# Delta-rule attention and a Mish layer on one core: heads paired over batches b and b+2, attention stages of half a chunk in five bundles, and TensorE's order written out

## The chip, the cores and the metric

The kernel runs on one core of one Trainium2 chip. The metric is the device time of one execution in microseconds. Before the change the median of three runs is 741.32 us (740.75 to 742.46). The profiled execution has a span of 745.6 us.

The engines are named as in the profile: PE is TensorE (matrix products; PEld are its weight loads), DVE is VectorE, ACT is ScalarE, POOL is GpSimd and SP is SyncE, which issues the DMAs.

## The reference, cut to what matters

```python
# q, k, v: (4, 8, 768, 48) float32, beta: (4, 8, 768); batch, head, token, dimension
k_n = k / (np.linalg.norm(k, axis=-1, keepdims=True) + 1e-06)
state = zeros((B, H, D, D))
for t in range(S):
    y[:, :, t] = einsum('bhd,bhde->bhe', q[:, :, t], state)
    v_old = einsum('bhde,bhd->bhe', state, k_n[:, :, t])
    state = state + beta[:, :, t, None, None] * einsum('bhd,bhe->bhde', k_n[:, :, t], v[:, :, t] - v_old)

x = y.transpose(0, 2, 1, 3).reshape(4 * 768, 8 * 48)      # 3072 tokens of 384
h = x @ w_in                                              # 384 x 2048
sp = where(h > 20, h, log1p(exp(minimum(h, 20))))
out = (h * tanh(sp)) @ w_out                              # 2048 x 384
```

The weights come as float64. The first part is a recurrence over the tokens for each of 32 heads of a batch; the second works on each token alone.

## The kernel before, in words

**Chunks.** The 768 tokens are cut in 12 chunks of 64. A chunk has 4 batches x 64 = 256 tokens for the Mish layer. Layer n, on chunk n, runs while the attention of chunk n+1 runs; the y of chunk n+1 has to be complete when layer n+1 begins.

**The layer** (`moe`) makes eight pieces g1 and eight pieces g2. A g1 is 18 products into an h tile of 128x512 in PSUM (line L505; 128x256 a product, in float32r with high and low parts), and then a chain: exp on ACT (L509), add on DVE (L510), square, log and exp on ACT (L511 to L513), a scalar-tensor-tensor e<-e,h on DVE (L514, the last reader of h), a cast to g on ACT (L522) and the low part of g on DVE, or on POOL in the first three layers (L525). A g2 is 12 products of 128x384 into two accumulators (L535) and comes two pieces after its g1. The h tiles have two buffers in PSUM, so an h begins when e<-e,h of the h before the last one is done. At a layer's end `turn` transposes the next chunk's y to x (L481, L483, L484).

**The attention of a chunk** (`step`) has five stages. Two heads side by side share every instruction; before the change these are heads 2p and 2p+1 of one batch, and a stage works on one batch (PB = 4 pairs).

- s1: v scaled on POOL (L361), q transposed on DVE (L372), products gq with K and the state (64x64 tiles, L381), v less a part of them (L386), another part masked into xx (L389)
- s2: za = T~ times v for the first 32 tokens (32x32 tiles, L398), copied to xx on ACT (L403)
- s3: pr (32x32, L413), v less pr on DVE (L419)
- s4: zb as za, for the other 32 tokens
- s5: py and ps, the output y and the new state (128x64 and 128x48, L431 and L437), copied out on ACT (L446, L447); the next chunk's k is loaded into xx

The four batches go through the stages one behind the other. All small PSUM tiles come from a pool `at` with four buffers.

**The early part of a group of two chunks** (`early`): K transposed on DVE (L216), Gram blocks pg on PE (64x32, L235), a forward substitution of 31 steps on DVE (L290, L295; for group 1 the first 18 steps are on POOL), which gives T~ in tt (L301). Stages s2 and s4 read tt.

**What sets the order.** `plan` gives each piece a time in units of a layer; pieces are emitted in the order of their times, and a scheduler then orders each engine's instructions by its own estimate of time, unless they stand within `manual_schedule` for that engine. `m0, m1` bound the stretch of times that does; with (9, 9) it is empty.

Of the kernel before, what the change touches and what calls it, by code (L numbers as in the profile page):

```python
# [16 lines left out]
# float32 values whose bits are 0x38000000 and 0x47EFFFFF: the high words of float64s of  # L17
# float32's least and largest exponent
# [15 lines left out]
def kernel(  # L34
# [32 lines left out]
    P = 128  # L67
# [3 lines left out]
    PB = NP // B  # L71
# [5 lines left out]
    kk = k.rearrange("b (p hh) t d -> hh t (b p) d", hh=2)  # L77
    qq = q.rearrange("b (p hh) t d -> hh t (b p) d", hh=2)
    vv = v.rearrange("b (p hh) t d -> hh t (b p) d", hh=2)
    bt = beta.rearrange("b (p hh) (g t2 c i) -> hh c t2 (b p) g i", hh=2, t2=2, c=2, i=32)  # L80
# [20 lines left out]
    # lmask[p, f] = f >= p % 32 ; amask[(hh,c,j), i] = i > 32c + j  # L101
# [21 lines left out]
    # parts of the weights, each first as float64 and then, in the same place, as high and low parts  # L123
# [47 lines left out]
    def convert(kind, i):  # L171
# [5 lines left out]
        # magnitudes outside float32's exponents go to 0 or the largest  # L177
        # and 2^-80 of the rest has bits that, moved up by 3, are float32's of -|w|
# [5 lines left out]
        # the sign comes by VectorE or, while VectorE is what holds the start up, by the others  # L184
# [18 lines left out]
    kts, tts, nes, ats, vts, dts, tus, yms = {}, {}, {}, {}, {}, {}, {}, {}  # L203

    def early(g):
# [3 lines left out]
        for t2 in range(2):  # L209
# [57 lines left out]
        # N[i, j] = -G[i, j] b'_j ; X = (I - N)^-1 in place  # L267
# [42 lines left out]
    def merge(n):  # L310
        """T~'s rows 16.. and columns ..15 of each block of 32: -T~22 G21 T~11."""
# [39 lines left out]
    def load_k(n, b):  # L351
        for hh in range(2):
            load(xx[b][64 * hh:64 * hh + 64, :, hh, D + C:], kk[hh, C * n:C * n + C, PB * b:PB * b + PB])

    def step(n, y):
        g, t2 = n // 2, n % 2
        kt, at, ne = kts[n], ats[n], nes[g]

        def scale_v(b):
            vt = vts[n, b // 2][:, PB * (b % 2):PB * (b % 2) + PB, :]  # L360
            nc.gpsimd.tensor_tensor(out=vt, in0=vt,  # L361
                                    in1=bcast_in(ne[:, 16 * t2 + PB * b:16 * t2 + PB * b + PB], D), op=ALU.mult)

        def s1(b, half=None):
            pr = slice(PB * b, PB * b + PB)
            p8 = slice(PB * (b % 2), PB * (b % 2) + PB)
            vt, x = vts[n, b // 2], xx[b]
            if n:
                scale_v(b)
            for hh in range(2 if half != 1 else 0):  # L370
                r = slice(64 - 64 * hh, 128 - 64 * hh)
                queue(nc.vector.transpose(x[r, :, hh, D:D + C], qsrc[r, pr].rearrange("p a b c -> p a (b c)")), n == 0)  # L372
            if half == 0:
                return
            # S is 0 in the first chunk
            d = D if n else 0
            ps = pa.tile([P, PB, C + d], F32, tag="at", name=f"gq{n}_{b}")
            for p in range(PB):
                for hh in range(2):
                    r = slice(64 - 64 * hh, 128 - 64 * hh)  # L380
                    m = nc.tensor.matmul(ps[64 * hh:64 * hh + 64, p, :], kt[r, PB * b + p], x[r, p, hh, D - d:D + C],  # L381
                                         start=True, stop=True)
            if n == 0:
                keep_warm(TN.get('wgq', 1), m)
            if n:
                nc.vector.tensor_tensor(out=vt[:, p8, :], in0=vt[:, p8, :], in1=ps[:, :, 0:D], op=ALU.subtract)  # L386
            for hh in range(2):
                r = slice(64 * hh, 64 * hh + 64)
                queue(nc.vector.tensor_tensor(out=x[r, :, hh, D:D + C], in0=ps[r, :, d:],  # L389
                                              in1=bcast_mid(amask[r], PB), op=ALU.mult), n < QS)  # L390

        def solve(b, c):
            """Z~ of the chunk's tokens 32c.."""
            pz = pa.tile([P, PB, D], F32, tag="at", name=f"z{"ab"[c]}{n}_{b}")
            for p in range(PB):
                for hh in range(2):
                    r = slice(64 * hh + 32 * c, 64 * hh + 32 * c + 32)
                    m = nc.tensor.matmul(pz[r, p, :], tts[g][r, t2, PB * b + p, :],  # L398
                                         vts[n, b // 2][r, PB * (b % 2) + p, :], start=True, stop=True)
# [339 lines left out]
```

## Time and profile before

| what | us |
|---|---|
| median of three runs | 741.32 (740.75 to 742.46) |
| profiled execution, span | 745.6 |
| first h product of layers 0, 1, 2, 3 | 93.1, 163.5, 230.5, 289.1 |
| of layers 4 to 8 | 341.6, 393.9, 446.4, 498.6, 551.1 |
| of layers 9, 10, 11 | 602.0, 652.5, 700.3 |

The profiled execution is 4.3 us longer than the median. In the timeline a row is a run of equal instructions: start, duration from the first one's start to the last one's end, engine, line, operation, output<-inputs, tile of PE (rows x columns), shape, count, and in brackets the idle time before it and what ended it. A float32 product leaves two records, a float32r product one. In the rows that group a line, the numbers behind the bar are busy time, mean ns of one, idle time before them and its releasers.

### The profile page before, as it was taken

The page shows a single profiled execution, that of the slowest core. Times are in us where ns is not written, and L with a number is a line of the kernel's source. Part 1 is how long each engine was busy: PE and PEld are TensorE (multiplying, and loading weights), DVE is VectorE, ACT ScalarE, POOL GpSimd, SP SyncE. Part 2 cuts the span into 40 slices and gives each one's busy share as a digit, 9 for nine tenths or more (in the row PEclk, how much of TensorE's full clock was granted, in tenths as well). Part 3 has the DMA queues.
Part 4 walks back from the last instruction along what each step waited for, and adds up shares of the span by engine and source line. Part 5 has one row for each costly group of instructions (what it writes and reads, how often), then busy time and mean ns, then how long its engine had stood idle before and what let it go on. Part 6 is the DMA issues. An engine that isn't in the chain of part 4 may idle for free.

```text
span 745.6 us, 22768 instructions
## 1 busy us (share of the span) xinstructions
PE 682.3 (92%) x9656; PEld 602.3 (81%) x9674; DVE 534.3 (72%) x1152; ACT 468.9 (63%) x1005; POOL 127.4 (17%) x171
## 2 busy tenths in 40 slices
PE   5659699878799989999999999999999999999993
PEld 3236588768788878998898998998988989989993
DVE  5796999997747997659995579975499964454351
ACT  2233667755485666776776767767767767767681
POOL 3431336894221221000000000000000000000000
PEclk9756999789899999999999999999999999999998
DMA  5762910253213032122222221130130120000000
GB/s 87 185 181 40 380 32 7 30 84 60 25 32 59 8 54 48 21 44 50 37 34 41 40 38 34 24 51 15 24 59 14 33 49 18 18 23 1 17 7 21
DMA packets 160981, 37.75 MB, mean 51 GB/s; under 512 B 154224, under 2 KB 157296, under 8 KB 160880
## 3 DMA queue, kind: packets, MB, share of 16 engines
q1 hardware_dynamic: 160880, 36.30, 24.0%
q8 instruction: 76, 1.25, 0.7%
q14 instruction: 25, 0.20, 0.1%
HBM read 31.56 MB, written 4.72 MB: 49 GB/s over the span
## 4 chain that ended last, share of the span: by engine, by line
PE 67%; DVE 20%; SPq 4%; issue 3%; ACT 2%; DMA 2%; POOL 1%; DVEq 0%; POOLq 0%; ACTq 0%
PE h L505 24%; PE acc L535 22%; PE gq L381 4%; SPq L131 3%; PE py L431 3%; PE pg L235 2%; PE za L398 2%; DVE pr L290 2%; PE zb L398 2%; PE pr L413 2%; DVE gt L295 2%; PE warm L570 2%; PE ps L437 2%; DVE e L514 1%; DVE xx L389 1%
## 5 line engine op out<-in xcount | busy, mean ns | idle before, releaser
L505 PE MATMUL h<-x,wi 128*128 128x256 f32 x1728 | 238.3, 291 | 13.5 <-DVE e L514 12.1
L505 PEld LDWEIGHTS h<-x,wi 128*128 128x128 f32 x1728 | 218.4, 192 | 23.8 <-DVE e L514 12.5
L535 PE MATMUL acc<-wo,g 128*128 128x384 f32 x1152 | 233.4, 350 | 2.3 <-ACT g L522 1.9
L535 PEld LDWEIGHTS acc<-wo,g 128*128 128x128 f32 x1152 | 201.1, 192 | 8.8 <-ACT g L522 2.5
L514 DVE SCALAR_TENSOR_TENSOR e<-e,h 128x512 f32<-128x512 f32 x96 | 65.8, 685 | 45.5 <-ACT e L513 43.9
L522 ACT CAST g<-e 128x512 fp32r<-128x512 f32 x96 | 59.3, 618 | 49.6 <-DVE e L514 48.6
L361 POOL TENSOR_TENSOR vt<-vt,ne 128x192 f32<-128x192 f32 x48 | 27.3, 589 | 351.9 <-DMA vt<-in_v_dram 187.1
L509 ACT ACTIVATE e<-h 128x512 f32<-128x512 f32 x96 | 57.2, 596 | 47.9 <-PE h L505 45.2
L511 ACT ACTIVATE e<-e 128x512 f32<-128x512 f32 x96 | 60.5, 631 | 33.0 <-DVE e L510 32.5
L510 DVE TENSOR_SCALAR e<-e 128x512 f32<-128x512 f32 x96 | 42.7, 446 | 32.2 <-ACT e L509 31.0
L525 DVE TENSOR_TENSOR g<-e,g 128x512 fp32r<-128x512 f32 x72 | 49.1, 681 | 19.2 <-ACT g L522 18.6
L512 ACT ACTIVATE e<-e 128x512 f32<-128x512 f32 x96 | 60.5, 632 | 2.7
L513 ACT ACTIVATE e<-e 128x512 f32<-128x512 f32 x96 | 60.4, 631 | 2.4
L419 DVE TENSOR_TENSOR vt<-vt,pr 32x192 f32<-32x192 f32 x96 | 34.0, 354 | 32.7 <-PE pr L413 30.9
L290 DVE TENSOR_TENSOR pr<-gt 128x228 f32<-128x228 f32 (+14 forms) x147 | 53.9, 367 | 3.6 <-PE warm L292 0.5
L295 DVE TENSOR_TENSOR gt<-gt,pr 128x228 f32<-128x228 f32 (+14 forms) x147 | 51.5, 350 | 3.3
L372 DVE STREAM_TRANSPOSE xx<-qsrc 64x256 f32<-64x256 f32 x96 | 41.6, 437 | 13.9 <-PE ps L437 9.3
L381 PE MATMUL gq<-xx,kt 64*64 64x112 f32 (+1 forms) x768 | 47.6, 265 | 1.0 <-DVE x L484 1.0
L431 PEld LDWEIGHTS py<-xx 128*64 128x64 f32 x768 | 38.5, 138 | 10.7 <-issue 4.9
L431 PE MATMUL py<-xx 128*64 128x48 f32 x768 | 45.7, 227 | 1.0 <-ACT xx L403 0.3
L525 POOL TENSOR_TENSOR g<-e,g 128x512 fp32r<-128x512 f32 x24 | 31.9, 1328 | 74.1 <-ACT g L522 47.3
L381 PEld LDWEIGHTS gq<-xx,kt 64*64 64x64 f32 x768 | 37.4, 138 | 8.4 <-issue 4.5
(94 smaller groups left out, 838.3 us busy)
## 6 DMA issues: line engine op xcount, KB each, us to landing
ri<-in_moe_w_in_dram SPq DMA_DIRECT2D x12, 512.0 KB
ro<-in_moe_w_out_dram SPq DMA_DIRECT2D x16, 384.0 KB
vt<-in_v_dram SPq DMA_DIRECT2D x48, 96.0 KB
xx<-in_k_dram SPq DMA_DIRECT2D x96, 48.0 KB
out_dram<-o SPq DMA_DIRECT2D x24, 192.0 KB
qsrc<-in_q_dram SPq DMA_DIRECT2D x48, 64.0 KB
ksrc<-in_k_dram SPq DMA_DIRECT2D x44, 64.0 KB
qsrc<-in_q_dram SPq DMA_DIRECT2D x48, 32.0 KB
```

Of the source, the lines that this page charges most:

```text
L290: queue(eng.tensor_tensor(out=pv, in0=nj, in1=xj, op=ALU.mult), on)
L295: queue(eng.tensor_tensor(out=below, in0=below, in1=pv, op=ALU.add), on)
L381: m = nc.tensor.matmul(ps[64 * hh:64 * hh + 64, p, :], kt[r, PB * b + p], x[r, p, hh, D - d:D + C], start=True, stop=True)
L431: nc.tensor.matmul(py[64 * hh:64 * hh + 64, p, :], x[:, p, hh, D:D + C], x[:, p, hh, 0:D], start=True, stop=True)
L505: nc.tensor.matmul(h[:, f2, :], wt["i", f * P // WI * NCH + c][:, i2, f0:f0 + P], x[:, c, :], start=(i == 0), stop=(i == 3 * NCH - 1))
L511: nc.scalar.activation(e, e, AF.Square)
L512: nc.scalar.activation(e, e, AF.Ln, bias=0.5, scale=0.5)
L513: nc.scalar.activation(e, e, AF.Exp, scale=-1.0)
L514: nc.vector.scalar_tensor_tensor(e, e, -1.0, h, op0=ALU.add, op1=ALU.mult)
L522: nc.scalar.copy(out=gg[:, 0], in_=e)
L525: eng.tensor_tensor(out=gg[:, 1], in0=e, in1=gg[:, 0], op=ALU.subtract)
L535: nc.tensor.matmul(acc[t], gg[:, a, f2, ts_], wt["o", f][:, i2, :], start=(f == 0 and i == 0), stop=(f == NF - 1 and i == 2))
```

## The change

The rearranged inputs pair batch b with batch b+2, so that the row half of a tile is the batch's upper bit and a pair index runs over two batches and eight heads. A stage works on one of two halves h of a chunk, with eight pairs; there are two xx tiles of twice the width. The two heads of a pair are now in different rows of y as well, so y of a half is one tile that one copy of 128 rows takes out of PSUM. The copies, subtractions, transposes and loads of k become half as many, each twice as long; s1's products go to two tiles of four pairs each (gq_h0, gq_h1). The tiles of v have four buffers instead of three.

Stages are grouped in five bundles a chunk: s2 of half 0 with s1 of half 1; s3 with s2; s4 with s3; s5 with s4; and s5 of half 1 with s1 of half 0 of the next chunk. The loads of q and v, and the early part of a group, get earlier times, and the Gram pieces stand with the second and third bundle. From time 0.9 on PE issues as emitted.

```diff
-    PB = NP // B
+    PB = NP // 2
-    kk = k.rearrange("b (p hh) t d -> hh t (b p) d", hh=2)
+    kk = k.rearrange("(hh b) h t d -> hh t (b h) d", hh=2)
...
-    xx = [cp.tile([P, PB, 2, W], F32, name=f"xx{i}") for i in range(B)]
+    xx = [cp.tile([P, PB, 2, W], F32, name=f"xx{i}") for i in range(2)]
...
-            vt = vts[n, h8] = ap.tile([P, 8, D], F32, tag="vt", name=f"vt{n}_{h8}", bufs=3)
+            vt = vts[n, h8] = ap.tile([P, 8, D], F32, tag="vt", name=f"vt{n}_{h8}", bufs=4)
...
+        def s1(h):
+            vt, x, kt = vts[n, h], xx[h], kts[n]
+            if n:
+                scale_v(h)
+                turn_q(h)
+            d = D if n else 0
+            for h4 in range(2):
+                p4 = slice(4 * h4, 4 * h4 + 4)
+                ps = pa.tile([P, 4, C + d], F32, tag="at", name=f"gq{n}_{h}{h4}")
+                for p in range(4):
...
+        def s3(h):
+            pr = pa.tile([P, PB, D], F32, tag="at", name=f"pr{n}_{h}")
+            for p in range(PB):
...
+            for hh in range(2):
+                r = slice(64 * hh + 32, 64 * hh + 64)
+                vb = vts[n, h][r]
+                queue(nc.vector.tensor_tensor(out=vb, in0=vb, in1=pr[r], op=ALU.subtract), n < QS)
...
+            nc.scalar.copy(out=y[:, h, :].rearrange("r (p d) -> r p d", d=D), in_=py)
...
+            dst = out.rearrange("(hh b r) f -> b hh r f", hh=2, b=2)[t, :, C * n:C * n + C, :]
+            nc.sync.dma_start(out=dst, in_=o)
...
-            t0 = TN.get('p1', -1.2) if n == 0 else n - 0.3
+            t0 = TN.get('p1', -1.2) if n == 0 else 0.2 if n == 1 else 1.0 if n == 2 else n - 1.1
             put(one(prep, n + 1), 1, t0, t0)
-            t0 = TN.get('a1', -0.05) if n == 0 else TN.get('a2', 0.15) if n == 1 else -0.05
-            if n == 1:
-                attend2 = attend(2)
-                put(attend2, 4, TN.get('s2a', 1.0), TN.get('s2b', 1.1))
-                put(attend2, 16, 1 + t0, 1.78)
-            else:
-                put(attend(n + 1), 20, n + t0, n + 0.78)
+    at(-0.03, (1, S1, 0))
+    for n in range(1, NS):
+        ts = ([0.12, 0.25, 0.38, 0.51, 0.64] if n == 1 else [0.95, 1.1, 1.25, 1.4, 1.55] if n == 2 else
+              [n - 1 + t for t in (-0.13, 0.09, 0.27, 0.46, 0.65)])
+        at(ts[0], (n, S2, 0), (n, S1, 1))
+        at(ts[1], (n, S3, 0), (n, S2, 1))
+        at(ts[2], (n, S4, 0), (n, S3, 1))
+        at(ts[3], (n, S5, 0), (n, S4, 1))
+        at(ts[4], (n, S5, 1), (n + 1, S1, 0))
     for g in range(2, NS // 2):
         gen = early(g)
-        end = TN.get('e2', 1.2) if g == 2 else 2 * g - 3.1
+        end = TN.get('e2', 1.2) if g == 2 else 2 * g - 3.4
         put(gen, 1, end - TN.get('kl', 0.25), end - TN.get('kl', 0.25))
-        for t in TN.get('pp', [0, 0.05, 0.15, 0.25, 0.3, 0.4]):
+        for t in ((0, 0.151, 0.152, 0.2, 0.301, 0.302) if g == 2 else (0.1, 0.491, 0.492, 0.5, 0.671, 0.672)):
             put(gen, 1, end + t, end + t)
-        put(gen, 63, end + TN.get('pp', [0.4])[-1] + TN.get('ke', 0.02), 2 * g - 1.1)
-    m0, m1 = TN.get('m', (9, 9))
+        put(gen, 63, end + (0.35 if g == 2 else 0.7), 2 * g - 1.4)
+    m0, m1 = 0.9, 99
```

In the following rows `a<-b,c` is output<-inputs, the number behind a name is a buffer's, and x16 counts equal rows. PE in layer 4, from the end of h_1 or h_2 on; before, a batch's stages stand in many small pieces:

```order
L413 MATMUL pr_0_4887<-xx_98,at_2996 32x48 x8
L398 MATMUL za_1_4901<-vt_0_4609,tt_3914 32x48 x8
L381 MATMUL gq_2_4948<-xx_100,kt_2893 64x112 x8
L505 MATMUL h_2_4912<-x_4_4697,wi_845 128x256
...
L398 MATMUL zb_0_4975<-vt_0_4609,tt_3914 32x48 x2
L535 MATMUL acc_4_4806<-wo_576,g_0_4834 128x384 x2
...
L398 MATMUL zb_0_4975<-vt_0_4609,tt_3914 32x48 x6
L413 MATMUL pr_1_5018<-xx_99,at_2996 32x48 x4
L535 MATMUL acc_4_4806<-wo_576,g_0_4834 128x384
```

Now the same stages of layer 4 in the change:

```order
L482 MATMUL h_1_4715<-x_4_4559,wi_505 128x256
L417 MATMUL pr_0_4744<-xx_98,at_2733 32x48 x16
L402 MATMUL za_1_4763<-vt_1_3833,tt_3618 32x48 x16
L482 MATMUL h_2_4787<-x_4_4559,wi_827 128x256
...
L482 MATMUL h_3_4835<-x_4_4559,wi_827 128x256
...
L402 MATMUL zb_0_4866<-vt_0_3830,tt_3618 32x48 x16
L417 MATMUL pr_1_4885<-xx_99,at_2733 32x48 x16
L512 MATMUL acc_4_4680<-wo_619,g_1_4741 128x384 x3
```

Each stage is now one block of 16 products, two blocks stand together, and nothing of the attention stands within a g2.

PE where layer 0 passes into layer 1. Before:

```order
L481 MATMUL xt_1_2306<-ident,yy_1596 128x128 x3
L381 MATMUL gq_0_2328<-xx_98,kt_1207 64x112
...
L381 MATMUL gq_3_2431<-xx_101,kt_1207 64x112 x8
L505 MATMUL h_0_2399<-x_1_2298,wi_418 128x256
```

In the change:

```order
L512 MATMUL acc_0_1582<-wo_2008,g_7_2215 128x384 x3
L402 MATMUL za_0_2270<-vt_0_1768,tt_1955 32x48 x16
L385 MATMUL gq_10_2292<-xx_99,kt_1153 64x112 x8
L385 MATMUL gq_11_2304<-xx_99,kt_1153 64x112 x8
L482 MATMUL h_0_2347<-x_1_2230,wi_406 128x256
```

The block za_0 of chunk 2, which reads tt of group 1 (tt_1955), now stands ahead of the first h of layer 1.

DVE in the change at the start of layer 3, where the first e<-e,h of the layer (L491, which was L514) stands; L423 is the subtraction of pr, which was L419:

```order
L487 TENSOR_SCALAR e_0_3875<-e_0_3875 128x512
L423 TENSOR_TENSOR vt_0_3142<-vt_0_3142,pr_0_3914 32x384 x2
L487 TENSOR_SCALAR e_1_3904<-e_1_3904 128x512
L491 SCALAR_TENSOR_TENSOR e_0_3875<-e_0_3875,h_0_3856 128x512
L239 TENSOR_TENSOR d_3470<-pg_0_3953,lmask 128x256
```

Two subtractions, which wait for the block pr_0 on PE, and the add of the second h stand between the first add and the first e<-e,h.

More of the change, by code (lines that the diff above doesn't have):

```diff
@@ L355, in step, with steps @@
-    def step(n, y):
+            load(xx[h][64 * hh:64 * hh + 64, :, hh, D + C:], kk[hh, C * n:C * n + C, PB * h:PB * h + PB])
+    def steps(n):
         g, t2 = n // 2, n % 2
[L357 to L367, printed above, removed]
-            if n:
[L369 to L374, printed above, removed]
-            d = D if n else 0
-            ps = pa.tile([P, PB, C + d], F32, tag="at", name=f"gq{n}_{b}")
-            for p in range(PB):
-                for hh in range(2):
[L380 to L394, printed above, removed]
@@ new lines, in steps, with scale_v, turn_q @@
+        y = ys[n] = ap.tile([P, 2, DM], F32, tag="yy", name=f"yy{n}", bufs=1)
+        def scale_v(h):
+            nc.gpsimd.tensor_tensor(out=vts[n, h], in0=vts[n, h],
+                                    in1=bcast_in(nes[g][:, 16 * t2 + PB * h:16 * t2 + PB * h + PB], D), op=ALU.mult)
+        def turn_q(h):
+            pr = slice(PB * h, PB * h + PB)
+            for hh in range(2):
+                r = slice(64 - 64 * hh, 128 - 64 * hh)
+                queue(nc.vector.transpose(xx[h][r, :, hh, D:D + C], qsrc[r, pr].rearrange("p a b c -> p a (b c)")),
+                      n == 0)
@@ L395, in solve @@
+        def solve(h, c):
+            pz = pa.tile([P, PB, D], F32, tag="at", name=f"z{"ab"[c]}{n}_{h}")
             for p in range(PB):
@@ L578 @@
     ys, xs = {}, {}
-    def attend(n):
-        ys[n] = ap.tile([P, B // 2, DM], F32, tag="yy", name=f"yy{n}", bufs=1)
-        yield from step(n, ys[n])
     def turn(n):
@@ L592 @@
     plan = []
+    SCALE, TURN, S1, S2, S3, S4, S5 = range(7)
     def put(gen, n, t0, t1):
@@ L606 @@
         nc.gpsimd.memset(t, 0.0)
-    q0, last, wz = [], [], TN.get('wz', [1] * 4)
+    last = []
     def load_beta():
@@ L629, in loads @@
             elif x == "x":
-                for b in range(B):
-                    load_k(0, b)
+                for h in range(2):
+                    load_k(0, h)
             else:
@@ L642, with at, run, warmed @@
     put(one(loads, TN.get('d1', ["q", "v", 2, "k2", 2, "k3", 2, "x", 22])), 1, -2.901, -2.901)
-    put(attend0, 1, -2.3, -2.3)
+    chunk = {}
+    def at(t, *work):
+        def run():
+            for n, i, h in work:
+                if n < NS:
+                    if n not in chunk:
+                        chunk[n] = steps(n)
+                    chunk[n][i](h)
+            yield
+        put(run(), 1, t, t)
+    def warmed(t, n, i, h):
+        def run():
+            chunk[n][i](h)
+            keep_warm(8, last[-1])
+            yield
+        put(run(), 1, t, t)
+    at(-2.3, (0, SCALE, 0), (0, SCALE, 1))
     put(one(loads, TN.get('d2', [28])), 1, TN.get('p1', -1.2) + 0.001, TN.get('p1', -1.2) + 0.001)
@@ L653 @@
         put(merge(3), 4, t0 + TN.get('md', 0.3), t0 + TN.get('md', 0.3) + 0.1)
[L654 to L659 removed]
+    for i, (t0, t1) in zip((S2, S3, S4, S5), TN.get('st')):
+        for h in range(2):
+            warmed(t0 + (t1 - t0) * h / 2, 0, i, h)
+    for h in range(2):
+        at(-1.95 + 0.05 * h, (0, TURN, h))
+        at(-1.6 + 0.05 * h, (0, S1, h))
     put(early1, 6, TN.get('k2a', -2.5), TN.get('k2b', -2.0))
```

109 lines of the change are left out of this document (37 added, 72 removed).

## The prediction

> **What bounds the kernel now.** I read the page first (busy time per engine and the chain of waits), then the table of windows from one layer's first h product to the next one's, then PE's waits and its timeline. Page:
>
> ```profile
> span 745.6 us, 22768 instructions
> PE 682.3 (92%) x9656; PEld 602.3 (81%) x9674; DVE 534.3 (72%) x1152; ACT 468.9 (63%) x1005; POOL 127.4 (17%) x171
> PE 67%; DVE 20%; SPq 4%; issue 3%; ACT 2%; DMA 2%; POOL 1%; DVEq 0%; POOLq 0%; ACTq 0%
> ```
>
> 92% is an average over two regimes. The windows, one row per layer from layer 0 on (columns: stretch, length, busy PE, PEld, DVE, ACT, POOL, then granted clock, DMA share, GB/s):
>
> ```profile
> 93.10:163.50 70.40, 59.87 (x929) 53.29 (x927) 67.58 (x125) 48.65 (x107) 46.35 (x55) 0.91 0.25 38
> 163.50:230.50 67.00, 60.49 (x862) 56.16 (x862) 41.87 (x81) 39.15 (x86) 20.91 (x21) 0.91 0.26 42
> 230.50:289.10 58.60, 54.10 (x714) 47.56 (x710) 55.31 (x123) 35.92 (x79) 13.95 (x15) 1.00 0.24 39
> 289.10:341.60 52.50, 52.50 (x813) 47.99 (x807) 32.51 (x72) 37.56 (x82) 2.14 (x5) 1.00 0.22 37
> 446.40:498.60 52.20, 52.03 (x712) 46.97 (x710) 48.27 (x118) 35.81 (x76) 2.48 (x4) 1.00 0.19 34
> 498.60:551.10 52.50, 52.50 (x813) 47.99 (x807) 30.94 (x70) 37.56 (x82) 2.10 (x5) 1.00 0.16 30
> 551.10:602.00 50.90, 50.52 (x633) 45.72 (x632) 46.67 (x116) 35.30 (x75) 2.12 (x4) 1.00 0.17 32
> 602.00:652.50 50.50, 50.50 (x631) 45.85 (x630) 24.25 (x51) 36.51 (x77) 0.97 (x2) 1.00 0.14 26
> 652.50:700.30 47.80, 47.80 (x553) 43.57 (x552) 22.69 (x47) 33.07 (x67) 0.00 (x0) 1.00 0.03 9
> ```
>
> From 289.1 on PE is never free for more than 0.4 us in a layer: those layers cost what PE's own sequence costs. Layers 0 and 2 are DVE's (67.58 of 70.40, 55.31 of 58.60), and layer 1 holds the waits:
>
> ```profile
> PE h L505 <- DVE e L514: 10.4, 3, 5.5
> 188.43 1.25 DVE L216 STREAM_TRANSPOSE kt<-ksrc 128x1024 f32<-128x1024 f32 x1 [6.95 <-DMA ksrc<-in_k_dram]
> 198.50 2.09 DVE L301 STREAM_TRANSPOSE tt<-gt 128x1024 f32<-128x1024 f32 x1
> ```
>
> **What a change of tile size costs PE.** The attention runs on 32x32, 64x64 or 128x48 pieces, the layer on 128x128. First rows: inside the interleaved order of layer 3; last three: the undisturbed last layer (start, duration).
>
> ```profile
> 314.57 0.40 PE L398 MATMUL zb<-vt,tt 32*32 32x48 f32 x10
> ...
> 314.93 0.38 PE L413 MATMUL pr<-xx,at 32*32 32x48 f32 x10
> 315.24 2.40 PE L505 MATMUL h<-x,wi 128*128 128x256 f32 x18
> 317.56 1.10 PE L235 MATMUL pg<-kt 64*32 64x64 f32 x64
> 318.59 0.53 PE L398 MATMUL za<-vt,tt 32*32 32x48 f32 x16
> 319.05 2.38 PE L535 MATMUL acc<-wo,g 128*128 128x384 f32 x12
> 321.36 0.32 PE L431 MATMUL py<-xx 128*64 128x48 f32 x4
> ...
> 710.97 2.25 PE L535 MATMUL acc<-wo,g 128*128 128x384 f32 x12
> 713.05 2.30 PE L505 MATMUL h<-x,wi 128*128 128x256 f32 x18
> 715.19 4.33 PE L535 MATMUL acc<-wo,g 128*128 128x384 f32 x24
> ```
>
> Start to start, 18 h take 2.32 here (315.24 to 317.56) and 2.14 there; 12 acc take 2.31 and 2.08. So a visit between two visits of small tiles is 0.18 to 0.23 longer, 0.205 in the mean. The last pr starts at 314.93 + 0.38 − 0.20 (one small product lasts 0.20 by these rows' neighbours) = 315.11, and the first h 0.13 later, where small ones follow each other by 0.02: +0.11. One trip from big tiles to small and back costs 0.31. The Trainium skill, "TensorEngine Tiling (Array Packing)", Tiling Modes, Key Properties, says that a change of tiling mode drains TensorE; it gives no figure, and these rows agree with it.
>
> **Layers 3 to 8, part by part.** Two layers (446.4 to 551.1) last 104.7, and PE leaves the big tiles 32 times in them (first 446.4, last 551.1, counted in the timeline). The change's order leaves them 5 times a layer: 22 trips fewer, −6.8.
>
> Against this, alternating zb and pr products overlap (an fp32 product leaves two records, counted here): 32 records last 314.57 to 315.11, 17 ns each, while za alone goes from 318.59 to 318.59 + 0.53 − 0.20 = 318.92 for 15 steps, 22 ns each. Full blocks of 16 lose this: 5 ns x the 128 zb and pr records of a layer, +0.65, so +1.3 for two; gq runs twice as long give back about 0.2. The number of products is unchanged. 104.7 − 6.8 + 1.3 − 0.2 = 99.0.
>
> Then a wait that wasn't there. h has two buffers, so h_2 needs e<-e,h (stt) of h_0. The chain is shown undisturbed in the last layer:
>
> ```profile
> 723.59 2.30 PE L505 MATMUL h<-x,wi 128*128 128x256 f32 x18
> 725.93 0.60 ACT L509 ACTIVATE e<-h 128x512 f32<-128x512 f32 x1 [1.17 <-PE h L505]
> 729.01 0.69 DVE L514 SCALAR_TENSOR_TENSOR e<-e,h 128x512 f32<-128x512 f32 x1 [1.25 <-ACT e L513]
> L419 DVE TENSOR_TENSOR vt<-vt,pr 32x192 f32<-32x192 f32 x64 | 22.6, 354 | 25.3 <-PE pr L413 24.3
> L484 DVE TENSOR_TENSOR x<-xt,x 128x384 fp32r<-128x384 f32 x16 | 8.6, 549 | 5.6 <-ACT x L483 5.6
> L510 DVE TENSOR_SCALAR e<-e 128x512 f32<-128x512 f32 x64 | 27.1, 423 | 19.3 <-ACT e L509 18.3
> ```
>
> From the end of an h (725.89) to the end of its stt (729.70) pass 3.81. In the change h_1 and the bundle pr_0, za_1 stand between h_0 and h_2: PE is through 1.98 (h_1: 2.14 less the 0.16 by which an h starts ahead of the modelled end of the one before it, 713.05 + 2.30 against 715.19) + 0.09 (exit, by the rows above) + 1.41 (two blocks of 32 records at 22 ns) + 0.11 = 3.6 after h_0. DVE now has two vt<-vt,pr and e_1's add ahead of that stt. pr_0 is done at 1.98 + 0.09 + 0.70 + 0.20 = 2.97; vt<-vt,pr of 32x384 isn't in the trace: not under 0.354 (the 32x192 form), not over 0.55 (128x384); I take 0.55, the row of equal length per partition. 2.97 + 2 x 0.55 + 0.42 (e_1's add) + 0.69 = 5.2, so PE waits 1.6, or 1.9 where a solve step of DVE also stands between (1.2 at the lower bound). In layers 3, 5 and 7 two pg blocks stand there too (64 records each, 317.56 to 318.59, about 0.95 without the exit), and the wait is nil. One wait for each pair: +1.8.
>
> A wait can lower the clock:
>
> ```profile
> 131.90:135.30 3.40, 1.75 (x65) 1.49 (x61) 3.33 (x5) 2.34 (x6) 3.05 (x5) 0.99 0.16 27
> 135.30:138.70 3.40, 3.40 (x14) 2.90 (x11) 3.37 (x4) 2.03 (x4) 2.44 (x3) 0.51 0.03 7
> 275.20:278.60 3.40, 1.67 (x10) 1.25 (x8) 3.20 (x9) 3.29 (x9) 0.67 (x1) 1.00 0.32 58
> ```
>
> 1.65 idle with small products beside it was followed by a stretch at 0.51; 1.73 idle with big ones (the third row) wasn't. The new waits stand between the two (small products, then idle, then big ones). A stretch at half clock loses 1.7; at a chance of 0.4, +0.7 each. The Trainium skill, "TensorE: Matmul & The Clock Gate", Part 1, lets the clock fall after an idle window of about 3.4 us; by it waits of under 2 cost no clock and the sum would be 4 us lower, some 725. The row at 131.9 speaks against it.
>
> A pair comes to 99.0 + 1.8 + 0.7 = 101.5. Layers 3 to 8 last 312.9 (289.1 to 602.0) and three pairs 304.5: **−8.4** (the third pair gains less, since its layer 8 has few pg records before). Layer 9: 11 trips −3.4, +0.65 −0.1 +1.6 +0.7 = **−0.55**. Layer 10, 10 trips: **−0.25**. In the last layer h_3 comes before any acc and waits for stt of h_0: **+0.4**, estimated from the chain of 3.81 less h_1 and h_2.
>
> **Edits at nothing.** Wider ACT copies (96 of 64x192 for y become 24 of 128x384, the za, zb and ps copies half as many), wider transposes of qsrc, half the k loads on SP: about 39 us less on ACT and 15 on DVE. They lie under PE from layer 3 on, where ACT is busy 33 to 38 of 50 us and DVE at most 48; without that cover they would be gains only. The loads of q, v and ksrc stand about a chunk earlier on SP, behind fewer k loads. The solve is spread over 1.3 layers.
>
> **The start.** Layers 0 to 2 end at 289.1. The change's PE order puts za_0 of chunk 2, which needs tt of group 1, ahead of h_0 of layer 1; before, layer 1 began at 163.5 while that solve still ran. What counts is when tt comes. On DVE 20 rows fewer stand ahead of the solve's b' scaling (L278), 15 fewer between it and pr_18 and 33 fewer ahead of tt. At 0.35 to 0.44 each (rows above) that is about 8 for the first lot, and DVE has no slack in layer 0. Some 20 us of DVE work then remain behind pr_18. tt comes at about 180 instead of 200.6 (5 either way). From there layer 1 lasts 51.4 (half a pair, 49.5, and half of what its four pg blocks of 0.95 make it dearer than its neighbour, 1.9) + 1.6 for the wait + 2.5 for the low clock after the idle time: it ends at 235.5. Layer 2: 47.6 + 1.6 + 0.7 = 49.9, so layer 3 starts at 285.4. DVE was nearly full in layer 2, so I take 286: **−3** (6 either way).
>
> **Sum.** −3 −8.4 −0.55 −0.25 +0.4 = −11.8 on a span of 745.6: 733.8. The profiled execution's span is 4.3 over the median of the runs, 741.32, so the time is 729.5: I say 729.
>
> **Rivals.**
> A. The new wait is absent, since stt_0 is issued earlier than its order suggests or vt<-vt,pr is at its lower bound, and the clock holds. Then 3 x 2.5 and 2 x 2.3 are gained: 717. For: 3.81 of undisturbed chain is near PE's 3.6. Against: DVE issues in order.
> B. The clock falls at every wait, for two stretches (3.4 instead of 0.7), in layers 2, 4, 6, 8, 9, 10: +16, 745, slower than before. It decides from a loss of 2.0 a wait more than I took (11.8/6). For: the row at 135.3. Against: the one at 275.2.
> C. PE is held at za_0 of chunk 2: tt comes at 195 and not at 180, since the solve, which DVE shares with layer 0, is bound by POOL's part of it, and layer 1 follows whole: +15, 744. It decides from tt at 192. For: tt is at 198.5 before, and PE then had 37 us of layer 1 beside it. Against: DVE's rows ahead of it are fewer.
> D. The trips aren't on the path (the switches hide under weight loads) and only the start moves: 738 to 741. Against: PE has no idle time in these layers.
>
> **How the numbers follow.** Forecast 0.57 (own range 721 to 737), A 0.15, B 0.11, C 0.12, D 0.05. The range, 713 to 745, takes in A's lower end and the larger part of B and C. Under 0.2% (1.5 us) is taken for no change: faster 0.75 (nearly all of the forecast, A, and little of the others), same 0.07 (D, the edges of B and C), slower 0.18.
>
> **What would show it.** In the profile after: windows from layer 3 on of 50 to 51.5 us each; PE's waits with h from e<-e,h of 1.6 to 1.9, five or six times; the same timeline rows with 2.14 and 2.08 within runs; tt<-gt ending at 175 to 185; a granted clock under 1.00 in few windows after 240. Layers as long as before, or h waiting in all of them, would make it wrong.

## The result, and the profile after

The change makes the kernel slower: 752.32 us in the median of four runs (750.35 to 754.24) against 741.89 of the kernel before (740.75 to 742.55). The ratio is 1.0132, with a 95% interval from 1.0088 to 1.0176. 729 was forecast. Here and below, medians and ranges are of the executions within 1.5% of the fastest of their kernel; one execution each of e2, e3 and e4 lies above that.

The page of the kernel after, busy time by engine and the chain of waits:

```profile
span 752.5 us, 22310 instructions
PE 664.9 (88%) x9674; PEld 609.4 (81%) x9674; DVE 520.6 (69%) x1052; ACT 427.5 (57%) x793; POOL 122.3 (16%) x145
PE 52%; DVE 30%; ACT 6%; issue 5%; SPq 3%; DMA 2%; POOL 1%; DVEq 0%; ACTq 0%; POOLq 0%
```

PE is busy for 17 us less than before and idle for 24 us more. DVE has 30% of the chain that ended last, where it had 20%: work went off PE as meant, and PE waits for DVE instead.

The profile of the kernel before that the prediction used had a late start. A second one (e11, below) has a span of 739.7. Its windows, for layer 0, 1, 2, then layers 3 to 8 and 9 to 10 together (columns as in the prediction):

```profile
86.50:157.40 70.90, 58.60 (x928) 52.30 (x926) 68.07 (x126) 48.56 (x106) 47.01 (x55) 0.91 0.23 34
157.40:224.90 67.50, 60.15 (x863) 55.11 (x863) 42.03 (x81) 39.38 (x86) 20.84 (x21) 0.91 0.25 41
224.90:283.20 58.30, 53.90 (x712) 47.54 (x710) 55.01 (x123) 36.03 (x79) 14.11 (x15) 1.00 0.24 39
283.20:596.20 313.00, 312.11 (x4475) 283.67 (x4470) 238.95 (x560) 220.05 (x473) 13.44 (x27) 1.00 0.20 36
596.20:694.50 98.30, 98.30 (x1182) 89.41 (x1181) 46.97 (x97) 69.70 (x144) 0.97 (x2) 1.00 0.09 18
```

The same stretches of the kernel after:

```profile
83.70:184.70 101.00, 74.83 (x985) 67.25 (x983) 89.06 (x157) 49.31 (x97) 55.79 (x63) 0.77 0.27 40
184.70:245.70 61.00, 55.17 (x888) 52.61 (x887) 42.18 (x91) 33.09 (x63) 12.24 (x11) 0.93 0.18 28
245.70:296.80 51.10, 48.46 (x633) 46.70 (x632) 34.56 (x69) 32.32 (x58) 12.02 (x10) 0.97 0.24 40
296.80:611.70 314.90, 300.82 (x4549) 287.08 (x4549) 233.35 (x511) 197.75 (x366) 11.09 (x15) 0.98 0.20 36
611.70:707.40 95.70, 91.67 (x1102) 88.09 (x1101) 42.24 (x76) 62.35 (x110) 0.00 (x0) 0.96 0.05 14
```

Layer 3 begins at 296.8 instead of 283.2, 13.6 later; from the first h of layer 0 on, which began 2.8 earlier, it is 213.1 instead of 196.7. Layers 3 to 8 take 314.9 instead of 313.0, 1.9 more, and what follows (140.8 against 143.5) takes 2.7 less. The sum is 12.8, the difference of the two spans. (The medians differ by 10.4; the profiled execution is the slowest of the change's four, 754.24.) So the loss is at the start, and the gain expected of the later layers is missing. PE's waits after, in layers 1 and 2 and then from layer 3 on (waited for, in total, times, longest):

```profile
PE h L482 <- DVE e L491: 4.1, 2, 2.6
PE acc L512 <- ACT g L499: 3.4, 1, 3.4
PE acc L512 <- POOL g L502: 0.9, 1, 0.9
...
PE h L482 <- DVE e L491: 12.8, 6, 3.0
PE gq L385 <- DVE x L461: 2.6, 2, 1.8
PE acc L512 <- ACT g L499: 1.4, 2, 1.0
PE acc L512 <- DVE g L502: 0.8, 1, 0.8
```

From layer 3 on h had waited 0.6 us in all, for x; now PE is idle for 17.6, nearly three quarters of it at h for e<-e,h.

**Where it waits.** PE's timeline of layer 9, which has no solve and no Gram pieces:

```profile
611.72 4.48 PE L482 MATMUL h<-x,wi 128*128 128x256 f32 x36
616.13 0.74 PE L417 MATMUL pr<-xx,at 32*32 32x48 f32 x26
...
616.83 0.72 PE L402 MATMUL za<-vt,tt 32*32 32x48 f32 x26
619.49 3.69 PE L482 MATMUL h<-x,wi 128*128 128x256 f32 x18 [1.95 <-DVE e L491]
622.98 2.52 PE L512 MATMUL acc<-wo,g 128*128 128x384 f32 x12
...
619.49:622.98 3.49, 3.49 (x19) 3.49 (x19) 1.77 (x3) 2.29 (x4) 0.00 (x0) 0.59 0.07 28
```

h_0 and h_1, the two blocks, 1.95 idle, and then an h_2 that takes 622.98 − 619.49 = 3.49 instead of 2.14. The last row is the window of this h_2: the clock granted over it is 0.59, 1.00 up to 620.1 and 0.51 from there to 623.6. The same stands in layers 2, 4, 6, 8 and 10.

**At the start** (DVE's and PE's timelines):

```profile
163.94 0.67 DVE L491 SCALAR_TENSOR_TENSOR e<-e,h 128x512 f32<-128x512 f32 x1
...
165.32 4.89 PE L512 MATMUL acc<-wo,g 128*128 128x384 f32 x15 [8.70 <-ACT g L499]
...
178.09 1.90 DVE L301 STREAM_TRANSPOSE tt<-gt 128x1024 f32<-128x1024 f32 x1
...
180.09 1.49 PE L402 MATMUL za<-vt,tt 32*32 32x48 f32 x32 [5.17 <-issue]
181.51 3.25 PE L385 MATMUL gq<-xx,kt 64*64 64x112 f32 x32
184.69 5.38 PE L482 MATMUL h<-x,wi 128*128 128x256 f32 x36
...
192.91 3.33 PE L482 MATMUL h<-x,wi 128*128 128x256 f32 x16 [1.49 <-DVE e L491]
```

tt of group 1 ends at 180.0, as forecast. PE stood idle for it (the row of za names no releaser, but za begins 0.1 after tt ends), does the first bundle at a granted clock of 0.50 in 4.6 us, and begins layer 1 at 184.7; the kernel before, in e11, began it at 157.4 and worked on it while the solve ran. Its tt came here:

```profile
192.82 2.06 DVE L301 STREAM_TRANSPOSE tt<-gt 128x1024 f32<-128x1024 f32 x1
```

Counted from the first h of layer 0, tt comes after 96.3 us in the change (180.0 − 83.7) and after 108.4 in e11 (194.9 − 86.5). The longest wait of PE in layer 0 is another one: 8.70 us at acc for a g, whose chain has rows of the weights' conversion and of the solve between its steps on DVE (its e<-e,h begins at 163.94). It is there in e3 too (8.70), and shorter in e6 (6.38); no run takes it away, so its price is open.

**In the solve's layers** (DVE, layer 5 and then layer 7):

```profile
423.36 2.07 DVE L246 STREAM_TRANSPOSE gt<-d 128x1024 f32<-128x1024 f32 x1
...
428.33 1.74 DVE L273 TENSOR_TENSOR gt<-gt,nb 128x1024 f32<-128x1024 f32 x1
...
430.98 0.42 DVE L487 TENSOR_SCALAR e<-e 128x512 f32<-128x512 f32 x1
...
533.17 0.15 DVE L280 STREAM_TRANSPOSE ne<-ss 128x32 f32<-128x32 f32 x1
533.25 0.38 DVE L487 TENSOR_SCALAR e<-e 128x512 f32<-128x512 f32 x1
533.54 0.18 DVE L265 SCALAR_TENSOR_TENSOR nb<-rc 128x32 f32<-128x32 f32 x1
```

The row at 430.98 is the add of e_4. In layer 5 the whole preparation of the solve and its first two steps (four rows) stand ahead of that add; in layer 7 the scheduler put it earlier, between L280 and L265. Layer 5 takes 55.2 us, layer 3, with the same order as layer 5, 54.5, and layer 7 51.6.

This gives three suspects: the wait at h_2 with the half clock behind it, the solve's place on DVE in layers 1, 3 and 5, and the hold of PE at the start.

### The profile page after: what moved, and what is told of

Read it like the earlier page. It is cut to its first block, busy times and chain, and to the rows that moved or that the text cites. A ratio compares the mean times of both kernels' runs of the same rounds, so it can differ in the third digit from the quotient of the medians.

```text
span 752.5 us, 22310 instructions
## 1 busy us (share of the span) xinstructions
PE 664.9 (88%) x9674; PEld 609.4 (81%) x9674; DVE 520.6 (69%) x1052; ACT 427.5 (57%) x793; POOL 122.3 (16%) x145
## 4 chain that ended last, share of the span: by engine, by line
PE 52%; DVE 30%; ACT 6%; issue 5%; SPq 3%; DMA 2%; POOL 1%; DVEq 0%; ACTq 0%; POOLq 0%
PE h L482 21%; PE acc L512 18%; DVE gt L295 4%; DVE pr L290 4%; SPq L131 3%; DVE e L491 3%; PE gq L385 3%; DVE xx L393 2%; PE py L435 2%; DVE e L487 2%; DVE xx L369 2%; PE warm L542 2%; PE zb L402 1%; DVE vt L423 1%; PE pr L417 1%
## 5 line engine op out<-in xcount | busy, mean ns | idle before, releaser
L482 PEld LDWEIGHTS h<-x,wi 128*128 128x128 f32 x1728 | 227.6, 200 | 28.2 <-issue 20.7
L512 PE MATMUL acc<-wo,g 128*128 128x384 f32 x1152 | 230.7, 349 | 17.4 <-ACT g L499 13.5
L512 PEld LDWEIGHTS acc<-wo,g 128*128 128x128 f32 x1152 | 204.3, 194 | 24.5 <-ACT g L499 15.0
L491 DVE SCALAR_TENSOR_TENSOR e<-e,h 128x512 f32<-128x512 f32 x96 | 65.8, 686 | 63.6 <-ACT e L490 60.7
L362 POOL TENSOR_TENSOR vt<-vt,ne 128x384 f32<-128x384 f32 x24 | 21.6, 905 | 304.0 <-DMA vt<-in_v_dram 182.3
L385 PE MATMUL gq<-xx,kt 64*64 64x112 f32 (+1 forms) x768 | 47.6, 276 | 2.6 <-DVE x L461 2.6
L385 PEld LDWEIGHTS gq<-xx,kt 64*64 64x64 f32 x768 | 41.0, 146 | 5.7 <-DVE x L461 3.0
L435 PE MATMUL py<-xx 128*64 128x48 f32 x768 | 41.9, 226 | 0.4 <-ACT xx L407 0.4
L393 DVE TENSOR_TENSOR xx<-gq,amask 64x256 f32<-64x256 f32 x96 | 40.2, 418 | 0.8
L542 PE MATMUL warm<-zero 128*128 128x512 bf16 (+1 forms) x128 | 38.0, 439 | 2.7 <-DVE zero L535 2.7
```

Of the source, the lines that this page charges most:

```text
L435: m = nc.tensor.matmul(py[64 * hh:64 * hh + 64, p, :], x[:, p, hh, D:D + C], x[:, p, hh, 0:D], start=True, stop=True)
L482: nc.tensor.matmul(h[:, f2, :], wt["i", f * P // WI * NCH + c][:, i2, f0:f0 + P], x[:, c, :], start=(i == 0), stop=(i == 3 * NCH - 1))
L491: nc.vector.scalar_tensor_tensor(e, e, -1.0, h, op0=ALU.add, op1=ALU.mult)
L512: nc.tensor.matmul(acc[t], gg[:, a, f2, ts_], wt["o", f][:, i2, :], start=(f == 0 and i == 0), stop=(f == NF - 1 and i == 2))
```

## The experiments

All of them start from the change, but for e10 and e11. Medians of their runs, the change being at 752.3 and the kernel before at 740.6 to 741.4 beside them.

### e1: 12 big products between h_1 and the blocks

```diff
+            if not acc:
+                acc.extend(po.tile([P, DM], F32, tag=f"acc{t}", name=f"acc{t}_{n}") for t in range(NTT))
...
-        put(moe(n, lambda n=n: turn(n + 1)), 18 + (n == NS - 1) * (TN.get('lag', 3) - 2), n, n + 1)
...
+            put(gen, 16, n, n + 16 / 18)
+            put(gen, 2, n + 1.085, n + 1.087)
```

> The change, with the last g2 of layers 1 to 10 and its output put behind h_1 of the next layer, so 12 acc products (2.1 us) stand between h_1 and the block pr_0, za_1. The wait theory (h_2 waits for e<-e,h of h_0 for 2.0 to 3.0 us in layers 2, 4, 6, 8, 9, 10, and each wait is followed by a stretch at half clock that costs 1.7): the wait and the low clock go in all six, about 25 us off the change's 752.3: 724 to 732. The rival (DVE and ACT are late in these layers anyway, and the wait only moves to the next h or acc): under 8 us off, 744 or more.

Measured: 732.5 us (728.9 to 733.0), 20 off the change and just above the 724 to 732 expected; ratio to the kernel before 0.987 (0.982 to 0.992). Layers 9 and 10 have no wait left and take 46.8 and 41.2 instead of 50.4 and 45.3 (10 is shorter also because its last g2 now stands in layer 11). PE's waits from 280 to 680:

```profile
PE h L481 <- DVE e L490: 5.7, 3, 3.1
PE gq L385 <- DVE x L461: 2.7, 2, 1.9
```

The wait theory holds for most of it. What stays at h stands in layers 4, 6 and 8, in which a solve runs on DVE.

### e2: PE not held at the start

```diff
-        ts = ([0.12, 0.25, 0.38, 0.51, 0.64] if n == 1 else [0.95, 1.1, 1.25, 1.4, 1.55] if n == 2 else
+        ts = ([0.12, 0.25, 0.38, 0.51, 0.64] if n == 1 else [1.1, 1.25, 1.4, 1.5, 1.65] if n == 2 else
```

The load of chunk 3's q stands ahead of the second half of chunk 2 here, and that half takes chunk 3's q, so the output is not the reference's; the instructions are the same.

> The change, with the five bundles of chunk 2 later (the first between h_1 and h_2 of layer 1), so that h_0 of layer 1 no longer stands behind za_0, which needs tt of group 1. If it is this hold that makes the start longer (5.2 us idle before za_0, 3 us of slow gq ahead of h_0, and a half clock until 193.4): first h of layer 1 at about 176 to 178 and 6 to 10 us off: 742 to 746. The rival (DVE's solve sets the pace of the start, and layer 1 ends when it did): layer 2 starts within 2 us of 245.7 and the time is 750 to 753.

Measured: 747.8 us (743.1 to 753.1), between the two expectations. Layer 1 begins at 174.3 instead of 184.7 and layer 2 at 240.6 instead of 245.7; half of the 10 us is given back in layer 1, in which the bundle of za_0 and gq now stands (4.6 us, 182.7 to 187.3) with a wait of 3.4 for tt ahead of it. Layer 3 begins 7.0 earlier. In the profiled run layers 3 and 7 took 56.2 and 56.4, and in both the scheduler had put e_4's add behind the solve's preparation: layers 3, 5 and 7 came to 164.2 instead of 161.3, which hides part of the gain. The start is part of the loss, with a size that this run alone doesn't settle.

### e3: the solve's preparation behind e_4's add

```diff
+            ads[n, fp] = nc.vector.tensor_scalar(e, e, EXP20, 1.0, op0=ALU.min, op1=ALU.add)
...
+        if g > 1:
+            order(nbi, ads[(1, 5) if g == 2 else (2 * g - 3, 4)])
...
-        put(gen, 63, end + (0.35 if g == 2 else 0.7), 2 * g - 1.4)
+        put(gen, 63, end + (0.37 if g == 2 else 0.77), 2 * g - 1.4)
```

The pieces of the solve are also emitted a little later (last two lines).

> The change, with one more rule of order on DVE: in the solve of groups 2 to 5 the first step that makes b' stands behind the add of e_5 (group 2) or e_4 (groups 3 to 5), as the scheduler already put it in layer 7. If layers 3 and 5 are 3 us longer than layer 7 because some 8 us of the solve's preparation stand ahead of that add: layers 3 and 5 come down to 51.5 to 52, layer 1 by 2 to 4: 8 us off, 743 to 746. The rival (DVE is full in these layers whatever the order, 43 us of 54.5 with a solve in the second half): layers 3 and 5 stay above 54 and the time within 2 us of 752.

Measured: 743.2 us (738.5 to 746.6). Layers 3, 5 and 7 take 51.5, 52.4 and 51.7, as the theory said, and layer 1 55.2 instead of 61.0, more than the 2 to 4 expected. That the order is the cause is also seen where no one asked for it: in e2 and e4 the scheduler's order came out one way or the other in layers 3, 5 and 7, and their times follow it: 56.2, 51.6 and 56.4 in e2, whose layer 5 has the add early, and 51.6, 55.7 and 51.5 in e4, whose layer 5 has it late.

### e4: the wait filled with big products

```diff
+    def fill(n):
+        ps = pa.tile([P, DM], F32, tag="at", name=f"fill{n}")
+        for i in range(12):
+            nc.tensor.matmul(ps, xs[n - 1][0][:, 0, 0:P], wt["o", 0][:, 0, :], start=True, stop=True)
...
+        if n in (3, 5, 7, 9, 10, 11):
+            put(one(fill, n), 1, ts[1] + 0.001, ts[1] + 0.001)
```

> The change, with 12 products of 128x384 (2.1 us), whose result nobody reads, ahead of h_2 in layers 2, 4, 6, 8, 9, 10, where PE waits. If the half clock comes from the idle time, it is gone and the wait itself stays in length: 1.7 us x 6 = 10 off, 741 to 744, with a granted clock of 1.00 in these layers. The rival (the low stretch has another cause, or the wait was measured too long): the clock is still below 1.00 in them, and the time is 752 or, with 12 products added to the path, up to 764.

Measured: 741.8 us (738.6 to 749.6). PE in layer 9:

```profile
609.87 2.37 PE L674 MATMUL fill<-wo,x 128*128 128x384 f32 x12
612.08 2.30 PE L482 MATMUL h<-x,wi 128*128 128x256 f32 x18
614.22 2.27 PE L512 MATMUL acc<-wo,g 128*128 128x384 f32 x12
```

h_2 takes 612.08 to 614.22, 2.14 again, and the layer 49.0 instead of 50.4. None of the six layers has a stretch at half clock. Over the six layers the filled waits give 9.3 us back (1.3 to 2.4 each), and layer 3, by its order on DVE, 2.9. 12 products more made the kernel faster: here the half clock came with the idle time and not with the work.

### e5 and e6: the three together

e5 is e1 and e3. e6 also has the later bundles of e2, with the load of chunk 3 behind them (1.12 instead of 1.0).

> The late g2 of e1 and the solve's rule of order of e3 together. If the two costs are separate places: e1's 732.5 less what the solve's preparation still costs in its layers 1, 5 and 7 (about 5.5 + 0.5 + 3.5, against layers that e3 had at 51.5 to 52.4 and 55.2): 720 to 725. The rival (one of them covered the other): 729 or more.

> e5, and the bundles of chunk 2 later as in e2 (the load of chunk 3's q and v stands behind that chunk's second bundle here, at time 1.12 instead of 1.0). In e2 layer 1 began 10 us earlier than in the change and layer 2 5 us earlier. If that stays: layer 1 begins at 174 to 176 and the time is 715 to 720. The rival (DVE's solve of group 2 sets the end of layer 1 whatever stands ahead): within 1.5 us of e5.

Measured: e5 724.3 us (722.6 to 725.4), ratio to the kernel before 0.976 (0.970 to 0.981); e6 723.0 (721.4 to 725.9), 0.975 (0.970 to 0.980). The waits and the solve's order add up, as expected. e6 lies 1.3 below e5, inside the rival's bound. Its layer 1 begins at 184.0 and not at 174 to 176, but its layer 0 began late too, at 92.5 (83.4 in e2). In the profiled runs layer 3 begins 197.4 after layer 0 in e6 and 201.3 in e5, so the hold costs something there too, but in the times its price can't be told from none.

### e7: every bundle taken apart

```diff
-        at(ts[1], (n, S3, 0), (n, S2, 1))
+        at(ts[1], (n, S3, 0))
+        at(tz[1], (n, S2, 1))
```

This is done for all five bundles of chunks 3 to 11; `tz` holds the times `ts` plus 0.04 to 0.17. The second stage of the first bundle stands behind the next chunk's load here, and half 1 takes that chunk's q, so the output is not the reference's; the instructions are the same.

> e6 with each bundle of chunks 3 to 11 taken apart: its two stages stand in two places, so PE leaves the big tiles 60 times instead of 30 in layers 3 to 8, and 7 times more in layers 9 and 10. The trip theory (0.31 us a trip): 43 trips more with layer 2's, +11 to +14 over e6. The rival (PE drains at no cost of its own; the trips' price in the profile before was the interleaving): within 3 us of e6.

Measured: 723.8 us (723.1 to 724.1), 0.8 over e6, as the rival said in the total. But layer 9, in which neither kernel waits, in e6 and then in e7:

```profile
589.10:635.90 46.80, 46.80 (x632) 44.99 (x630) 24.70 (x47) 31.89 (x58) 0.00 (x0) 1.00 0.08 19
582.30:630.70 48.40, 48.40 (x637) 45.62 (x631) 24.59 (x46) 32.58 (x58) 0.00 (x0) 1.00 0.08 18
```

The windows are cut to tenths; from the first h to the next layer's (589.11 to 635.94, 582.34 to 630.65) it is 46.83 and 48.31. Five trips more cost 1.5 us, 0.30 each: the trip theory. (Layers 9 and 10 have 9 trips more, not the 7 expected.) Layers 3 and 7, in which neither waits either, say the same, with 50.69 and 52.14 each. Layers 3 to 8 take 302.0 against 299.2, 2.8 more for 30 trips, because e6 has 4.0 us of waits there and one stretch at half clock, and e7 has none: the stages, spread out, fill the time in which h_2 would wait. So the total hides two things of nearly the same size.

### e8 and e10: who writes PE's order

e8 is the change with the scheduler's order on PE; e10 is the kernel before with the written one.

```diff
-    m0, m1 = 0.9, 99
+    m0, m1 = 99, 99
```

> The change with PE's order left to the scheduler, as before the change (everything else as in the change). PE leaves the big tiles 35 times in layers 3 to 8 (30 in the change, 97 before), and in layers 4 and 9 the blocks zb_0 and pr_1 now stand with pr_0 and za_1 ahead of h_2, where the change waits. If the written-out order is what made the waits: 730 to 738. The rival (the waits come from the wider blocks in any order): 748 to 754.

> The kernel before, with PE's order as emitted from time 0.9 on and nothing else changed. Its written order puts pr_0 and za_1 (of four pairs) ahead of h_2 in layers 3 to 10, and gq_1 ahead of h_1. If the written order by itself makes waits that the scheduler fills: h waits 1 to 1.5 us in most layers, each with a low clock in part of them, and the time is 752 to 768. The rival (the waits need the wider blocks): 738 to 744.

Measured: e8 735.5 us (732.4 to 741.8), ratio to the kernel before 0.992 (0.988 to 0.996); e10 779.6 (776.4 to 782.0), ratio 1.051 (1.046 to 1.056), above what was expected. All that the change does but for its written order makes the kernel some 6 us faster; the written order alone costs 17 there, and 38 in the kernel before. PE's waits in the whole of e10:

```profile
PE h L505 <- DVE e L514: 20.6, 12, 7.8
...
PE xt L481 <- ACT yy L447: 9.2, 11, 2.1
PE za L398 <- DVE tt L301: 8.6, 1, 8.6
```

Two of these places are the change's too: h for e<-e,h in most layers, and za for tt at the start. xt at the end of each layer is a new one. Layer 3 begins at 304.3 there, 21 later than in e11, and layers 3 to 8 take 328.2 instead of 313.0. In e8 PE has no wait at h from 280 to 680: the scheduler puts zb_0 and pr_1 in ahead of h_2, where PE waits 4.6 us in eight small pieces for vt<-vt,pr instead.

Most of e8's gain is at the start, where layer 3 begins 199.2 us after layer 0 instead of 213.1. Its layers 3 to 8 take 311.0, only 3.9 less than the change's: from the four blocks in a row on the clock falls in layers 4, 6 and 8, for five stretches in all. The first of them, in layer 4 (columns as before):

```profile
345.80:349.20 3.40, 2.06 (x84) 1.66 (x74) 3.21 (x9) 3.28 (x7) 0.00 (x0) 1.00 0.34 74
349.20:352.60 3.40, 3.40 (x38) 3.19 (x32) 3.07 (x7) 3.09 (x6) 0.00 (x0) 0.50 0.37 73
```

### e9: the block behind h_2

```diff
-              [n - 1 + t for t in (-0.13, 0.09, 0.27, 0.46, 0.65)])
+              [n - 1 + t for t in (-0.13, 0.15, 0.27, 0.46, 0.65)])
```

> e6, with the bundle pr_0, za_1 of chunks 3 to 11 behind h_2 instead of ahead of it (the Gram pieces go with it). In e6 PE still waits 1.2 to 2.4 us for e<-e,h of h_0 at h_2 in layers 2, 4, 6 and 8, since the two vt<-vt,pr stand ahead of it on DVE. If that is the rest of the wait: it falls under 0.3 (h_1 and 12 acc, 4.1 us, against a chain of 3.8), its half clock too, and the time is 713 to 719. The rival (DVE's solve is late in these layers whatever stands ahead of h_2): 721 to 725.

Measured: 727.2 us (721.0 to 731.3), above both expectations; the theory fell. The waits at h_2 grew to 2.3 to 3.7 in layers 2, 4, 6 and 8. e<-e,h of h_0 ends at the same time in both (6.70 us after the end of h_0 in layer 4 of e6, 6.76 in e9), with vt<-vt,pr ahead of it or not. What stands ahead of the chain is seen in e6 at the start of layer 4, whose first h ends at 343.04 and its exp at 343.67:

```profile
344.51 1.25 DVE L217 STREAM_TRANSPOSE kt<-ksrc 128x1024 f32<-128x1024 f32 x1
345.68 0.36 DVE L294 TENSOR_TENSOR pr<-gt 128x234 f32<-128x234 f32 x1
345.96 0.42 DVE L490 TENSOR_SCALAR e<-e 128x512 f32<-128x512 f32 x1
```

The first add begins 2.9 us after h_0 instead of 0.67: the stage's own xx<-gq (to 344.48), a transpose of K and a row of the solve are ahead of it.

### e11: the kernel before, once more

> The kernel before, unchanged, for a second profile: the first one's span of 745.6 is 4.3 over the median. If what differs lies in the start, its layers 3 to 10 last what they did (312.9 for layers 3 to 8, within 0.5) and layer 3 begins 3 to 7 us earlier than 289.1; the rival: the layers differ by over 1 us in sum.

Measured: 741.8 us, span 739.7. Layers 3 to 8 take 313.0 (312.9 in the first profile), and layer 3 begins at 283.2 instead of 289.1. The difference was there when the first h began (86.5 instead of 93.1). The largest difference in SP's timeline is at the loads of v, issued from 59.10 on in 5.41 us here and from 60.84 on in 12.47 in the first profile; why they took longer is open.

### e12: e_0's chain ahead of the solve

```diff
+            if g > 2 and t2:
+                order(m, firsts[2 * g - 4])
...
+            if g > 1 and j == 18:
+                order(mul, firsts[2 * g - 2])
```

`firsts[n]` is e<-e,h of h_0 in layer n, m the second transpose of K of a group, and mul step 18 of a solve.

> e6, with two more rules of order on DVE in layers 2, 4, 6 and 8: the solve's step 18 and the second transpose of K stand behind e<-e,h of h_0 (in e6 one of each, and 2 to 5 rows more of the solve, stand ahead of it; the first add of the layer starts 2.9 to 3.4 us after h_0 there, and 0.67 in layers 9 and 10, which have no solve). If the rest of the wait at h_2 is that: e<-e,h of h_0 ends 1.5 to 2.5 us earlier, the waits of 1.2 to 2.4 at h_2 in layers 2, 4, 6 and 8 are gone or under 0.4, and the time is 715 to 719. The rival (the stages' own work on DVE, vt<-vt,gq and xx<-gq, is what stands ahead): the waits stay over 1 and the time is 721 to 725.

Measured: 715.3 us (710.9 to 719.5), ratio to the kernel before 0.964 (0.961 to 0.968). The chain's first add in layers 4, 6 and 8 begins 1.5 to 2.0 us after h_0, and e<-e,h ends at 4.9 to 5.5 instead of 6.7 to 7.2; what still stands ahead of that add in layer 4 is the stage's own xx<-gq. PE's waits from 280 to 680:

```profile
PE acc L524 <- DVE g L512: 1.3, 2, 0.9
PE gq L394 <- DVE x L470: 0.2, 1, 0.2
```

None at h is left from layer 3 on (layer 2 keeps 1.8). This version beats both kernels, by 25 and by 37 us.

## Why the prediction was wrong

**The trip from big tiles to small and back: right.** 0.31 was worked out and 0.30 measured in e7. The layers without their waits are even somewhat cheaper than forecast: layer 9 takes 46.8 in e6, where a pair was to average 99.0/2 = 49.5, with its dearer half at 51.4 and the other at 47.6. (Layer 10 lost 11 trips, 15 before and 4 after, and not 10.) By the Trainium skill ("TensorEngine Tiling (Array Packing)", Tiling Modes, Key Properties) a change of tiling mode drains TensorE; the runs agree, with 0.3 us a trip.

**The wait at h_2: right in place, too small in price.** It was put in layers 2, 4, 6, 8, 9 and 10, with none where Gram pieces stand, and this is where it is. In layers 9 and 10 it is 1.95 for 1.6, and the working holds: in layer 9 e<-e,h ends 5.31 after h_0 (5.2 forecast) and PE is through with the blocks after 3.50 (3.6). In layers 2, 4, 6 and 8 it is 2.6 to 3.0 for 1.6 to 1.9: I had let one solve step stand between, and the chain begins later than that, since DVE comes to the new layer with work left over (e9, e12). The chance of 0.4 for the half clock was too low: it fell behind all six waits. Rival B, one stretch lower at every wait, is what happened, with one stretch each and not two. For layers 4, 6 and 8 the waits cost 3 us and the clock 3 us more than the sum had, and in layer 5 a stretch at half clock came as well.

**The solve: put at nothing.** I costed the spread of the solve at nothing, with PE as its cover. In layers 3 and 5 its preparation stood ahead of e_4's add, and these layers took 54.5 and 55.2 instead of 51.4, and layer 1 came out 5.8 longer by the same cause (e3). The order of DVE's instructions was there to read before the run. I read it where the layer begins and didn't follow it to the solve.

**The start: this step failed most.** Layer 3 was forecast to begin at 286 and began at 296.8: the term of −3 came out as +13.6 against e11 (+7.7 against the first profile). The 10.8 between the two are 4.7 for the bundle ahead of h_0, which the sum left out (180.0 to 184.7, at half clock), 5.5 in layer 1, which took 61.0 instead of 51.4 + 1.6 + 2.5 = 55.5 (the solve's order again, 5.8 by e3), and 1.2 in layer 2, less the margin of 0.6.

That tt came at 180, as forecast, was luck. The first profile's layer 0 began at 93.1 and the change's at 83.7, with nothing in the sum for that. From the first h of layer 0 on, tt was forecast after 87 us and came after 96.3, and after 95.3 to 99.3 in every other run of the change; the kernel before has 107.5 and 108.4. So the rows taken from DVE brought tt forward by 11 to 12 us and not by 20.6, and 9.4 us were hidden by a start that happened to be early. Rival C, tt late and PE held for it, is thus in good part what happened, but not for its reason, POOL's part of the solve: from 83.7 to 180.0 DVE was busy for 88.0 of 96.3 us. C named as a point in its favour that PE had 37 us of layer 1 beside the solve before. The change's order took this cover away; where e2 gives it back, layer 2 begins 5 us earlier.

**The clock.** By the Trainium skill ("TensorE: Matmul & The Clock Gate", Part 1) the clock falls after an idle window of about 3.4 us, so waits of under 2 were to cost none. The rows decide against it: 1.95 idle, with small products ahead, was followed by a stretch at half clock.

**The total.** The layers from 3 on were to bring −9 and brought +1.9 −2.7; the start was to bring −3 and took 13.6. In layers 3 to 8 the solve's term at nothing is the larger error: layers 3, 5 and 7 took 161.3 against 3 x 51.4, 7.1 more, and layers 4, 6 and 8 153.6 against 3 x 50.1, 3.3 more. The range ended at 745, since B and C were priced one by one, and both happened in part. PE's written order, which can't give way to whatever is late, has a part in both: without it (e8) the start takes 14 less, and from layer 3 on no h waits. It isn't all of it, since e8's layers 3 to 8 also miss the forecast of 304.5, by 6.5, with waits and half clocks of their own. That they can be had for less is shown by e12, which keeps the written order and takes 295.1 for them.

## What to carry to other kernels

A written order on one engine takes away the scheduler's filling of waits (17 us here, 38 in the kernel before): before it is taken, the chain that frees each buffer has to be followed on every engine that has a part in it, to the instruction ahead of it in that engine's order. Gains from fewer changes of tile are real and small each; one wait with a half clock behind it (1.95 + 1.35 in layer 9) eats ten of them. A new wait is better filled with work that is due anyway than with products that nobody reads: the last g2 of ten layers, moved behind h_1 of the next layer, brought 20 us (e1), the other 9 (e4). And a time read off one profile is compared with another only from an event that both share, here the first h of layer 0.

## What the runs showed of the hardware

By the clock that each profile shows from 232 on (the change, e1 to e3, e5, e6, e9 and e12), it fell behind 30 of 34 waits of 1.67 to 3.74 us, and behind none of the four at h of 1.15 to 1.38 in e5 and e6. It also fell with almost no idle time. In e8, layer 10, PE's stretch from 653.0 has 0.43 idle and holds nearly only 32x32 products (za, zb, pr); the next one was granted 0.50:

```profile
653.00:656.40 3.40, 2.97 (x122) 2.64 (x117) 2.44 (x5) 3.08 (x7) 0.00 (x0) 1.00 0.13 50
656.40:659.80 3.40, 3.40 (x18) 3.34 (x16) 2.27 (x4) 2.59 (x5) 0.00 (x0) 0.50 0.08 27
```

So in this row, as in layers 4, 6 and 8 of e8, a run of small products went ahead of a half clock with less idle time than the waits have. How much of the array has to be in use, the runs don't tell; four blocks of 32 records one behind the other, with 0.43 idle, were enough. The clock's own part in the change's waits was 1.3 to 2.4 us a layer (e4).
